# A fused FFT filter and squared-ReLU feed-forward kernel: the last zeta tile split, its last rows read alone, a cast shared by three engines, and one more group in the plain product form

## The chip, the cores and the metric

The kernel runs on one core of a Trainium2 chip. The metric is the device time of one launch in microseconds (us). Inputs and the output lie in the chip's main memory (DRAM) in fp32; the kernel computes in fp16 with fp32 sums in PSUM. Below, PE is the matrix engine, PEld its weight loads, DVE the vector engine, ACT the scalar (activation) engine, POOL the GpSimd engine and SP the engine that issues most transfers (DMA).

## What is computed

```python
X = np.fft.rfft(x, axis=1)                       # x: 8 x 3008 x 256
y = np.fft.irfft(X * (filt_r + 1j*filt_i), n=3008, axis=1)
h = np.maximum(y.reshape(24064, 256) @ w_in, 0)  # w_in: 256 x 2048
out = (h * h) @ w_out                            # w_out: 2048 x 256
```

## The kernel before, in words

**The filter part** goes batch by batch (8 batches). The FFT of 3008 = 64 x 47 points is done as matmuls in stages. `unit_a` (line 332; for batch 0 `unit_a0` and `turn_u`) makes u; for batches 1 to 7 it is written to DRAM (`write_u`) and read back turned (`read_u`). `unit_b` (line 406) makes a spectrum tile and DVE multiplies it by the filter `sF` (line 421). `unit_p` (line 454; for batch 0 `unit_p0`, line 435) transforms back to "zeta", which is cast to fp16, written to DRAM (`dZ`) and read back by `read_z` (line 475) in four chunks c, into two tiles `zt` that take turns. `unit_y` (line 483) makes the tokens `yt` of the feed-forward part.

**The feed-forward part** goes through 47 groups of 512 tokens, in 8 slots each: a loop over s at line 809. In its slots 8g to 8g+7 group g runs `ffn_g1` (the first product: 4 matmuls of 128x512 a slot, line 527, followed by an ACT ReLU of 128x1024, line 531) and `ffn_sq` (DVE squares of 128x2048 every second slot, line 538). In the eight slots that follow, the second product is made in one of two forms. The plain form, `ffn_g2` and `ffn_out`, has per slot 8 matmuls of 128x256 (line 547) and two ACT copies of the result a group. The other form, used for the groups in `SEVEN` (line 806) and run one slot later, saves multiplications in the manner of Strassen and Winograd: 112 matmuls of 128x128 (`products`, line 642) on blocks and on sums of blocks. DVE makes four sums of 128x2048 a group (`sums`, lines 613 to 622) and adds three results (lines 657 and 663); ACT copies four. It needs four differences of blocks of w_out, made once by `make_t` (line 594) in slots 12 to 15.

**The order of the work.** Each engine takes its instructions in the order in which the program gives them; it is written out by hand. Lines 734 to 804 are the prologue: batch 0 through the filter up to the first `unit_y`. After it, `fft_plan` (line 668) lays the units of batches 1 to 7 onto half-slots of the loop, with due times in slots. SP's transfers keep their program order too: in the prologue the zeta writes (line 450), then `read_z(0, 0)` and `read_z(0, 1)`, then eight writes of u of batch 1, each put there by `unit_a(1, c)`, then `read_z(0, 2)`. POOL loads w_out (line 321) only after a tiny copy (line 792) that reads the first row of the first zt tile.

**The filter's way in.** The two parts of the filter come as fp32 of 128x3008; each is cast to fp16 in two halves by DVE and POOL (lines 756 and 763). `place_f` (line 269) turns four rows at a time into `sF` with matmuls and one or two casts. For the imaginary part its block 0 (`place_f(1, 0, ...)`, line 768) reads columns 0 to 1023 and 2240 to the end.

**PSUM** is shared by three tags of two buffers each: `psH` (1024 fp32 wide, two banks), `psF` and `psO` (512 wide, one bank each). A new tile of a tag waits until the tile two before it has been read out. `unit_b`, `unit_p` and (after the prologue) `unit_y` all take `psF`.

**The last zeta of batch 0.** `unit_p0(5)` makes four rows of 128 in one psH tile and casts them in three pieces (line 447): rows 0 and 1 by ACT, row 2 by ACT, row 3 by DVE, each followed by its write to DRAM. `unit_a(1, 0)` follows on PE. Before the first `unit_y` there are five matmuls that only fill time (line 799).

Of the kernel before, what the change touches and what calls it, by code (L numbers as in the profile page):

```python
# [22 lines left out]
QF = 3008  # L23
# [87 lines left out]
def kernel(  # L111
# [9 lines left out]
    nc = tc.nc  # L121
    B, S, D = x.shape
# [5 lines left out]
    NG = T // TG  # L128
# [28 lines left out]
    def psF(name):  # L157
        return pps.tile([128, 512], F32, tag="psF", name=name, bufs=2)

    def psO(name):  # L160
        return pps.tile([128, 2, 256], F32, tag="psO", name=name, bufs=2)

    def psH(name):
        return pps.tile([128, 2, 512], F32, tag="psH", name=name, bufs=2)
# [4 lines left out]
    def bank_pair(name):  # L169

        k = npair[0] % 4
        npair[0] += 1
        if k < 2:
            t = psH(name)
            return [t[:, 0, :], t[:, 1, :]], [(t, 0)]
        ts = [psF(f"{name}_{i}") if k == 2 else psO(f"{name}_{i}").rearrange("p a d -> p (a d)")
              for i in range(2)]
        return ts, [(t.unsqueeze(1), i) for i, t in enumerate(ts)]
# [5 lines left out]
    x16s, us, uts, prods, zes, zts, yts = {}, {}, {}, {}, {}, {}, {}  # L184
# [36 lines left out]
    def cast(eng, out, in_):  # L221
        (eng.copy if eng is nc.scalar else eng.tensor_copy)(out=out, in_=in_)
# [9 lines left out]
    f32s = []  # L232
# [17 lines left out]
    sSP = const.tile([128, NC, 128], F16, name="sSP")  # L250
# [12 lines left out]
    ps = psO("warm").rearrange("p a d -> p (a d)")  # L263
# [3 lines left out]
    f16s = []  # L267

    def place_f(im, k, *engs, rotate=False):

        if rotate:
            banks, groups = bank_pair(f"psf_{im}_{k}")
        else:
            t = psH(f"psf_{im}_{k}")
            banks, groups = [t[:, 0, :], t[:, 1, :]], [(t, 0)]
        for i in range(4):
            c = 4 * k + i
            e0, e1 = D * c, D * (47 - c)
            cuts = [0] + [d for d in range(1, D)
                          if (e0 + d) % QF == 0 or (c and (e1 + d) % QF == 0)] + [D]  # L280
            for d0, d1 in zip(cuts, cuts[1:]):
                o = banks[i // 2][:, (i % 2) * D + d0:(i % 2) * D + d1]
                low = divmod(e0 + d0, QF)
                up = divmod(e1 + d0, QF) if c else (0, QF + d0)
                for r, (q, a) in enumerate((low, up, low, up)):
                    nc.tensor.matmul(o[32 * r:32 * r + 32, :], sPF[:, q, :],
                                     f16s[0][:, im, a:a + d1 - d0], start=True, stop=True)
        for t, i in groups:
            n = t.shape[1]
            eng = engs[i % len(engs)]  # L290
            dst = sF[:, im, 4 * k + 2 * i:4 * k + 2 * i + 2 * n, :]
            src = t.rearrange("p t (a d) -> p (t a) d", d=D)
            if eng is nc.scalar:
                eng.activation(out=dst, in_=src, func=AF.Copy, scale=sign[:, 0:1] if im else 1.0)
            elif im:
                eng.tensor_scalar_mul(out=dst, in0=src, scalar1=sign[:, 0:1])
            else:
                eng.tensor_copy(out=dst, in_=src)
# [33 lines left out]
    def unit_a(b, c):  # L332

        pool, tag = (p_y, "yt") if (b, c) == (1, 3) else (p_u, "u")
        u = us[(b, c)] = pool.tile([112, 8, D], F16, tag=tag, name=f"u_{b}_{c}")
        ph = psH(f"psA_{b}_{c}")
        if b == 1 and c % 2:
            ps = [psO(f"psA_{b}_{c}_{h}").rearrange("p a d -> p (a d)") for h in range(2)]
        else:
            ps = [psF(f"psA_{b}_{c}_{h}") for h in range(2)]  # L340
        for i in range(2):
            for j in range(2):
                m = slice(4 * j + 2 * i, 4 * j + 2 * i + 2)
                for h in range(2):
                    p = slice(64 * h, 64 * h + N2)
                    o = ps[h] if i == 0 else ph[:, h, :]
                    nc.tensor.matmul(o[64 * j:64 * j + 64, :], sSA[p], x16s[(b, c)][p, m, :],  # L347
                                     start=True, stop=True)
        for h in range(2):
            o = u[:, h:h + 3:2, :]  # L350
            pv = ps[h][0:112, :].rearrange("p (e d) -> p e d", d=D)
            if h == 0 or b == 1:
                nc.scalar.copy(out=o, in_=pv)
            else:
                nc.vector.tensor_copy(out=o, in_=pv)
        o = u[:, 4:8, :].rearrange("p (e h) d -> p h e d", h=2)
        pv = ph[0:112].rearrange("p h (e d) -> p h e d", d=D)
        if b == 1:
            nc.vector.tensor_copy(out=o, in_=pv)
        else:  # L360
            nc.scalar.copy(out=o, in_=pv)
        if b == 1:
            write_u(b, c)
# [69 lines left out]
    sSPx = []  # L433

    def unit_p0(k):

        if k == 0:
            zes[0] = p_h2.tile([128, NC, D], F16, tag="h2", name="ze_0")
        ze = zes[0][:, 4 * k:4 * k + 4, :]
        ps = psH(f"psP_0_{k}")  # L440
        for i in range(4):
            c2 = 4 * k + i
            prod = prods[(0, c2 // 2)]
            for v, w in enumerate((sSP[:, c2, :], sSPx[c2 // 12][:, c2 % 12, :])):
                nc.tensor.matmul(ps[:, i // 2, (i % 2) * D:(i % 2) * D + D], w,
                                 prod[:, v, i % 2, :], start=(v == 0), stop=(v == 1))
        for i, (c0, c1) in enumerate(((0, 4),) if k < 5 else ((0, 2), (2, 3), (3, 4))):
            cast(nc.vector if i == 2 else nc.scalar, ze[:, c0:c1, :],
                 ps.rearrange("p t (a d) -> p (t a) d", d=D)[:, c0:c1, :])
            nc.sync.dma_start(  # L450
                out=dZ[0].rearrange("(s p) d -> p s d", p=128)[:, 4 * k + c0:4 * k + c1, :],
                in_=ze[:, c0:c1, :])
# [22 lines left out]
    def read_z(b, c, ks=(0, 1)):  # L475
        zt = ztiles[c % 2]
        v = dZ[b].rearrange("(q j) d -> q j d", j=NM)
        for k in ks:
            nc.sync.dma_start(out=zt[64 * k:64 * k + 48],
                              in_=v[48 * k:48 * k + 48, 8 * c:8 * c + 8, :])  # L480
        zts[(b, c)] = zt

    def unit_y(b, n):
# [101 lines left out]
    def make_t(k):  # L585

        w = sWout.rearrange("p (q e) c -> p q e c", e=2)
        b11, b12 = w[:, :, 0, 0:128], w[:, :, 0, 128:256]
        b21, b22 = w[:, :, 1, 0:128], w[:, :, 1, 128:256]
        if k == 0:  # L590
            sg["t"] = p_t.tile([128, 4, 8, 128], F16, tag="t", name="sT")
        t = sg["t"]
        i0, i1 = ((b12, b11), (b22, t[:, 0]), (b22, b12), (b21, t[:, 1]))[k]
        nc.vector.tensor_sub(out=t[:, k], in0=i0, in1=i1)
        sg["w"] = {1: b11, 2: b21, 3: b22, 4: t[:, 3], 5: t[:, 0], 6: t[:, 1], 7: t[:, 2]}
# [133 lines left out]
    def run(plan, s, place):  # L729
        for f, *a in plan.get(2 * s + place, ()):  # L730
            f(*a)
# [7 lines left out]
    for k in range(2):  # L739
        c = slice(12 * k, 12 * k + 12)  # L740
# [19 lines left out]
    turn_u(4, nc.scalar)  # L760
    turn_u(5, nc.vector)
    place_f(0, 0, nc.scalar, rotate=True)
    for eng, e in ((nc.vector, slice(0, 1504)), (nc.gpsimd, slice(1504, QF))):
        cast(eng, f16s[0][:, 1, e], f32s[1][:, e])
    place_f(0, 1, nc.vector, rotate=True)
    for k in (2, 3):
        place_f(0, k, nc.scalar, rotate=True)
    place_f(1, 0, nc.scalar, nc.vector, rotate=True)
    for k in range(6):
        if k % 3 == 0:  # L770
            sSPx.append(p_u.tile([128, 12, 128], F16, tag="u", name=f"sSPx_{k}"))
        c, o = slice(4 * k, 4 * k + 4), slice(4 * k % 12, 4 * k % 12 + 4)
# [22 lines left out]
    for c in range(4):  # L795
        unit_a(1, c)
    ps = psF("fill")
    for _ in range(5):
        nc.tensor.matmul(ps, zero, sSB[:, 0:4, :].rearrange("p a b -> p (a b)"),
                         start=True, stop=True)  # L800
# [2 lines left out]
    prologue[0] = False  # L803
    read_z(0, 2)

    SEVEN = range(1, NG - 1)
    work = fft_plan()

    for s in range((NG + 1) * SLOTS):
        g, k = divmod(s, SLOTS)  # L810
        if g < NG:
            ffn_g1(g, k)
        run(work, s, 0)
        if 12 <= s < 16:
            make_t(s - 12)
        if (s - 1) // SLOTS - 1 in SEVEN:
            products((s - 1) // SLOTS - 1, (s - 1) % SLOTS, s)
        if g > 0 and g - 1 not in SEVEN:
            ffn_g2(g - 1, k)
        run(work, s, 1)  # L820
        if g > 0 and g - 1 not in SEVEN:
            ffn_out(g - 1, k)
        if g - 1 in SEVEN:
            sums(g - 1, k)
        if g < NG:
            ffn_sq(g, k)
        while stores and stores[0][0] <= s:
            _, i, n, ost = stores.pop(0)
            store(i, n, 2, ost)
# [30 lines left out]
```

## Time and profile before

| | us |
|---|---|
| device time, median of 3 | 757.33 (755.15 to 759.18) |
| profiled execution, span | 754.4 |
| PE busy | 737.1 (98%) |
| DVE busy | 651.0 (86%) |
| ACT busy | 563.5 (75%) |
| POOL busy | 192.2 (25%) |

Busy time is what the profiler has recorded for an engine. The matmuls are pipelined, so that the record of one lies over the start of the next: 8 matmuls of line 547 show 1.04 us, and the next work starts 0.87 to 0.88 us after them. Where PE's work is counted below, the distance from start to start is used. An entry in square brackets in a timeline is the idle time ahead of it and what ended it.

### The profile page before, as it was taken

What the parts mean: (1) busy time and instruction counts of PE and PEld (TensorE: products, weight loads), DVE (VectorE), ACT (ScalarE), POOL (GpSimd) and SP (SyncE); (2) the same over time, 40 slices, a digit from 0 to 9 for tenths busy, and PEclk for the clock granted to TensorE, in tenths of its full rate; (3) what the DMA queues carried; (4) which work ended last, traced back from release to release, by engine and by line L of the source; (5) the groups of instructions that cost most, each with busy time, mean ns of one, the idle gap of its engine ahead of it and who ended that gap; (6) DMA issues with size and microseconds to landing.
All of it is one profiled execution on the core that took longest, in us unless ns stands there. A gap on an engine that the chain in (4) does not pass through costs nothing.

```text
span 754.4 us, 20080 instructions
## 1 busy us (share of the span) xinstructions
PE 737.1 (98%) x8455; PEld 535.6 (71%) x8455; DVE 651.0 (86%) x724; ACT 563.5 (75%) x805; POOL 192.2 (25%) x265
## 2 busy tenths in 40 slices
PE   7889999999999999999999999999999999999998
PEld 5536667767677777877778776787778777777776
DVE  5956998899899897999979998999989989888783
ACT  5876787787778777777777778777787777777773
POOL 2811650243222321232304224033311222000000
PEclk9999999999999999999999999999999999999999
DMA  9996898566795557656585646764447333321011
GB/s 348 309 200 183 146 178 245 142 120 120 162 237 111 104 120 183 173 106 137 103 226 124 125 98 138 231 128 101 105 118 203 73 82 88 100 85 43 29 58 56
DMA packets 103490, 106.34 MB, mean 141 GB/s; under 512 B 10352, under 2 KB 93552, under 8 KB 102248
## 3 DMA queue, kind: packets, MB, share of 16 engines
q1 hardware_dynamic: 83960, 81.83, 36.0%
q0 software_dynamic: 19296, 23.05, 21.6%
q8 instruction: 66, 1.08, 0.6%
q10 hardware_dynamic: 144, 0.18, 0.2%
q14 instruction: 24, 0.20, 0.1%
HBM read 57.80 MB, written 48.23 MB: 141 GB/s over the span
## 4 chain that ended last, share of the span: by engine, by line
PE 87%; DMA 6%; DVE 3%; ACT 1%; issue 1%; POOL 1%; SPq 0%; DVEq 0%
PE psH L527 40%; PE psX L642 20%; PE psY L642 16%; PE psY L497 3%; PE psB L412 2%; PE psP L461 2%; DMA f<-in_filt_i_dram 2%; PE psA L347 2%; DVE prod L421 1%; DMA zt<-dZ 1%; PE psO L547 1%; DMA prod<-prod 1%; DMA dZ<-ze 1%; DVE h L538 1%; DMA sC<-cC 1%
## 5 line engine op out<-in xcount | busy, mean ns | idle before, releaser
L531 ACT ACTIVATE h<-psH 128x1024 f16<-128x1024 f32 x376 | 385.4, 1026 | 161.1 <-PE psH L527 160.1
L527 PE MATMUL psH<-yt,sWin 128*128 128x512 f16 (+7 forms) x1728 | 387.0, 351 | 1.2 <-ACT h L531 0.4
L538 DVE TENSOR_TENSOR h<-h 128x2048 f16<-128x2048 f16 (+1 forms) x192 | 229.9, 1198 | 47.6 <-ACT h L531 45.1
L429 POOL DMA_DIRECT2D prod<-prod x168 | 138.8, 968 | 427.6 <-DVE prod L421 425.3
L527 PEld LDWEIGHTS <-sWin 128*128 128x128 f16 x1728 | 149.2, 98 | 90.4 <-issue 3.0
L642 PEld LDWEIGHTS <-sum 128*128 128x128 f16 x2880 | 177.4, 98 | 24.8 <-issue 5.3
L642 PEld LDWEIGHTS <-h 128*128 128x128 f16 x2160 | 132.6, 98 | 24.3 <-issue 5.3
L421 DVE TENSOR_TENSOR prod<-psB,sF 128x1024 f16<-128x1024 f32 x84 | 102.3, 1219 | 12.6 <-PE psB L412 12.5
L642 PE MATMUL psX<-sT,sum 128*128 128x128 f16 x1440 | 102.4, 219 | 0.0
L642 PE MATMUL psY<-sT,sum 128*128 128x128 f16 x720 | 69.7, 219 | 0.0
L195 POOL DMA_DIRECT2D x<-in_x_dram x64 | 55.9, 1045 | 0.5 <-PE psA L347 0.5
L616 DVE TENSOR_TENSOR sum<-sum,h 128x2048 f16<-128x2048 f16 x45 | 54.9, 1221 | 0.8
L642 PE MATMUL psY<-sWout,sum 128*128 128x128 f16 x720 | 54.7, 219 | 0.6 <-DVE bot L657 0.6
L642 PE MATMUL psY<-sWout,h 128*128 128x128 f16 x720 | 55.0, 219 | 0.0
L642 PE MATMUL psX<-sT,h 128*128 128x128 f16 x720 | 54.9, 219 | 0.0
L619 DVE TENSOR_TENSOR sum<-h 128x2048 f16<-128x2048 f16 x45 | 54.8, 1217 | 0.0
L622 DVE TENSOR_TENSOR sum<-h,sum 128x2048 f16<-128x2048 f16 x45 | 54.8, 1217 | 0.0
L613 DVE TENSOR_TENSOR sum<-h 128x2048 f16<-128x2048 f16 x45 | 54.7, 1216 | 0.0
L463 ACT CAST ze<-psP 128x512 f16<-128x512 f32 x84 | 49.1, 585 | 1.1 <-PE psP L461 0.9
L506 DVE CAST yt<-psY 128x376 f16<-128x376 f32 x62 | 33.7, 544 | 16.7 <-PE psY L497 16.5
L642 PE MATMUL psX<-sWout,h 128*128 128x128 f16 x720 | 47.7, 219 | 0.0
L497 PE MATMUL psY<-sC,zt 112*128 112x94 f16 x512 | 42.3, 204 | 1.8 <-DVE prod L421 1.2
(76 smaller groups left out, 557.2 us busy)
## 6 DMA issues: line engine op xcount, KB each, us to landing
zt<-dZ SPq DMA_DIRECT2D x64, 192.0 KB
dU<-u SPq DMA_DIRECT2D x56, 192.0 KB
prod<-prod POOLq DMA_DIRECT2D x168, 64.0 KB, 2.7
dZ<-ze SPq DMA_DIRECT2D x28, 384.0 KB
x<-in_x_dram POOLq DMA_DIRECT2D x48, 192.0 KB, 5.0
ut<-dU SPq DMA_DIRECT2D x7, 1024.0 KB
out_dram<-top SPq DMA_DIRECT2D x31, 128.0 KB
out_dram<-bot SPq DMA_DIRECT2D x31, 128.0 KB
```

Source lines behind the costliest of these rows:

```text
L195: nc.gpsimd.dma_start(out=t[64 * h + p0:64 * h + p1], in_=v[p0:p1, 8 * c:8 * c + 8, :])
L421: nc.vector.tensor_mul(out=prod[:, :, a:a + n, :], in0=ps.rearrange("p (a d) -> p a d", d=D)[:, a:a + n, :].unsqueeze(1) .to_broadcast([12 ...
L429: nc.gpsimd.dma_start(out=prod[64 * i:64 * i + 64, 0], in_=prod[64 - 64 * i:128 - 64 * i, 1], accum_op=mybir.AluOpType.add)
L497: nc.tensor.matmul(ps[:, 94 * jj:94 * jj + 94], zt[:, 4 * (g % 2) + jj, dt * 128:(dt + 1) * 128], sSY, start=True, stop=True)
L527: nc.tensor.matmul(ps[:, i, o:o + n], sWin[:, dt, jt * 128:(jt + 1) * 128], yts[b][:, dt, r:r + n], start=(dt == 0), stop=(dt == 1))
L531: nc.scalar.activation(out=h2[:, 2 * s:2 * s + 2, :], in_=ps, func=AF.Relu)
L538: nc.vector.tensor_mul(out=v, in0=v, in1=v)
L613: nc.vector.tensor_add(out=t, in0=a21, in1=a22)
L616: nc.vector.tensor_sub(out=t, in0=f[5], in1=a11)
L619: nc.vector.tensor_sub(out=t, in0=a11, in1=a21)
L622: nc.vector.tensor_sub(out=t, in0=a12, in1=f[6])
L642: nc.tensor.matmul(o[:, t, :], f[p][:, q, 128 * t:128 * t + 128], sg["w"][p][:, q, :], start=(m == 0 and p in (1, 2)), stop=(q == 7), skip ...
```

## The change

It has four parts.

1. **The last zeta in three tiles.** In `unit_p0(5)` the three pieces get PSUM tiles of their own: rows 0 and 1 a psH tile, rows 2 and 3 a psF tile each. Each piece's cast follows its own matmuls. As this takes two psF tiles, `unit_a(1, c)` swaps: even c now take psO, odd c psF.
2. **The last z rows alone.** `read_z(0, 0)` reads rows 0 to 47, 48 to 79 and 80 to 95 in three transfers. Only the last depends on what `unit_p0(5)` writes. The other reads stay in two.
3. **The imaginary filter's cast in three parts.** POOL's half (columns 1504 to 3007) is cut at 2496, and ACT casts the rest, between two of its `place_f` casts.
4. **Group 1 in the plain form.** `SEVEN` starts at 2, so that groups 0 and 1 use w_out itself. The four differences of `make_t` move from slots 12 to 15 to slots 20 to 23.

```diff
-        if b == 1 and c % 2:
+        if b == 1 and c % 2 == 0:
             ps = [psO(...) for h in range(2)]
         else:
             ps = [psF(...) for h in range(2)]
...
-        ps = psH(f"psP_0_{k}")
-        for i in range(4):
...
-        for i, (c0, c1) in enumerate(((0, 4),) if k < 5 else ((0, 2), (2, 3), (3, 4))):
-            cast(nc.vector if i == 2 else nc.scalar, ze[:, c0:c1, :],
-                 ps.rearrange("p t (a d) -> p (t a) d", d=D)[:, c0:c1, :])
+        pieces = ((0, 4),) if k < 5 else ((0, 2), (2, 3), (3, 4))
+        pss = []
+        for c0, c1 in pieces:
+            if c1 - c0 > 1:
+                ps = psH(f"psP_0_{k}").rearrange("p t (a d) -> p (t a) d", d=D)
+            else:
+                ps = psF(f"psP_0_{k}_{c0}").rearrange("p (a d) -> p a d", d=D)
+            pss.append(ps)
+            for i in range(c0, c1):
...
+        for i, (c0, c1) in enumerate(pieces):
+            cast(nc.vector if i == 2 else nc.scalar, ze[:, c0:c1, :], pss[i][:, 0:c1 - c0, :])
...
-        for k in ks:
-            nc.sync.dma_start(out=zt[64 * k:64 * k + 48],
-                              in_=v[48 * k:48 * k + 48, 8 * c:8 * c + 8, :])
+        for q0, q1 in ((0, 48), (48, 80), (80, 96)) if (b, c) == (0, 0) else ((0, 48), (48, 96)):
+            r = q0 + q0 // 48 * 16
+            nc.sync.dma_start(out=zt[r:r + q1 - q0], in_=v[q0:q1, 8 * c:8 * c + 8, :])
...
-    for eng, e in ((nc.vector, slice(0, 1504)), (nc.gpsimd, slice(1504, QF))):
+    for eng, e in ((nc.vector, slice(0, 1504)), (nc.gpsimd, slice(1504, 2496))):
         cast(eng, f16s[0][:, 1, e], f32s[1][:, e])
     place_f(0, 1, nc.vector, rotate=True)
-    for k in (2, 3):
-        place_f(0, k, nc.scalar, rotate=True)
+    place_f(0, 2, nc.scalar, rotate=True)
+    cast(nc.scalar, f16s[0][:, 1, 2496:QF], f32s[1][:, 2496:QF])
+    place_f(0, 3, nc.scalar, rotate=True)
...
-    SEVEN = range(1, NG - 1)
+    SEVEN = range(2, NG - 1)
...
-        if 12 <= s < 16:
-            make_t(s - 12)
+        if 20 <= s < 24:
+            make_t(s - 20)
```

More of the change, by code (lines that the diff above doesn't have):

```diff
@@ L439, in unit_p0 @@
         ze = zes[0][:, 4 * k:4 * k + 4, :]
-        ps = psH(f"psP_0_{k}")
-        for i in range(4):
[L442 to L446, printed above, removed]
-        for i, (c0, c1) in enumerate(((0, 4),) if k < 5 else ((0, 2), (2, 3), (3, 4))):
-            cast(nc.vector if i == 2 else nc.scalar, ze[:, c0:c1, :],
-                 ps.rearrange("p t (a d) -> p (t a) d", d=D)[:, c0:c1, :])
+        pieces = ((0, 4),) if k < 5 else ((0, 2), (2, 3), (3, 4))
[7 more added lines that the diff above has]
+            for i in range(c0, c1):
+                c2 = 4 * k + i
+                prod = prods[(0, c2 // 2)]
+                for v, w in enumerate((sSP[:, c2, :], sSPx[c2 // 12][:, c2 % 12, :])):
+                    nc.tensor.matmul(ps[:, i - c0, :], w, prod[:, v, i % 2, :],
+                                     start=(v == 0), stop=(v == 1))
+        for i, (c0, c1) in enumerate(pieces):
+            cast(nc.vector if i == 2 else nc.scalar, ze[:, c0:c1, :], pss[i][:, 0:c1 - c0, :])
             nc.sync.dma_start(
```

## The prediction

> **What bounds the kernel now.** I first read the page's shares, then busy time by stretch, to see where PE has slack.
>
> ```profile
> core 0: us, PE busy (x) PEld busy (x) DVE busy (x) ACT busy (x) POOL busy (x), PEclk, DMA share, GB/s
> 44.00:62.00 18.00, 16.08 (x104) 8.26 (x102) 9.09 (x10) 11.40 (x14) 2.01 (x3) 0.94 1.02 200
> 62.00:76.00 14.00, 13.77 (x111) 9.33 (x110) 9.87 (x13) 9.37 (x13) 4.26 (x6) 1.00 0.63 177
> 76.00:103.00 27.00, 24.97 (x268) 17.60 (x266) 26.52 (x27) 20.19 (x31) 16.67 (x23) 1.00 0.90 162
> 103.00:120.00 17.00, 17.00 (x194) 11.32 (x193) 14.77 (x17) 15.05 (x23) 5.39 (x8) 1.00 0.91 202
> ```
>
> From 103 us PE is full, and it stays so (100.00 of 100.00 us in each stretch of 100 from 200 to 700). So only what happens ahead of 103 us can be gained, and PE work added anywhere is paid. Ahead of 103 there are two losses. From 76 to 103 DVE is the full engine. Before 62 a chain of waits binds; the chain by time for 36 to 63 shows it:
>
> ```profile
> 38.67 0.39 PE psP L445 x2
> ...
> 39.09 0.86 ACT ze L222 x2
> 39.95 0.50 ACT u L353
> 40.45 0.34 SPq L450
> ...
> 40.88 1.83 DMA dZ<-ze
> ...
> 42.80 3.24 DMA zt<-dZ
> ...
> 46.18 0.33 PE psY L497 x4
> ...
> 55.05 7.25 DMA zt<-dZ
> ```
>
> The last zeta's casts begin only when its last matmul is done, its third piece is written at 40.88, and the last read of z (192 KB) takes 3.24 us after that. The same chain starts, in time order from 0, with the imaginary filter landing at 20.77, then POOL's cast to 23.05. The timelines of POOL, DVE and PE give the rest:
>
> ```profile
> 15.65 1.44 POOL L222 CAST f<-f 128x1504 f16<-128x1504 f32 x1 [2.21 <-DMA f<-in_filt_r_dram]
> 20.82 2.21 POOL L222 CAST f<-f 128x1504 f16<-128x1504 f32 x1 [3.73 <-DMA f<-in_filt_i_dram]
> 39.98 0.43 DVE L222 CAST ze<-psP 128x256 f16<-128x256 f32 x1 [1.36 <-ACT ze L222]
> 43.29 2.32 PE L799 MATMUL fill<-sSB,zero 128*128 128x512 f16 x5
> 60.32 1.03 PE L547 MATMUL psO<-sWout,h 128*128 128x256 f16 x8 [0.48 <-DMA sWout<-in_moe_w_out_dram]
> 82.44 0.33 PE L497 MATMUL psY<-sC,zt 112*128 112x94 f16 x4 [1.01 <-DVE prod L421]
> ```
>
> POOL's second cast is 0.77 longer than its first, the third zeta piece waits for ACT's cast of the second, and at 82.44 PE stands waiting for a DVE product.
>
> [...] rows 2 and 3 share a bank, and DVE waited 1.36. [...] the 64 KB write of zeta took 1.83 on SP's. [...] Here the clock is 0.50 in each us from 43 to 46, and the five fill matmuls take 2.32.
>
> **The change part by part.**
>
> *Filter cast, −0.5.* POOL's 992 columns cost 1.44 x 992/1504 = 0.95, after the same 0.77 wait: done at 22.54, not 23.03. ACT's 128x512 is not in the trace from SBUF; the nearest row, from PSUM, is 0.59, and two full rows would be 1.03 at most. It queues behind `place_f(0,2)`'s cast and ahead of `place_f(0,3)`'s, so ACT reaches `place_f(1,0)` at 20.43 + 0.97 + 0.5 + 0.97 = 22.87 (start to start), against 23.42 before. DVE and ACT then run without gaps to 38 us, so 0.5 is passed on (0.3 with the dearer ACT cast).
>
> *Zeta tiles, −1.3.* Rows 0 and 1 (matmuls at 37.48) and row 2 (38.08) are cast while PE does row 3 (38.67 to 39.05); DVE casts row 3 at 39.09 and not 39.98. Its write is issued near 39.55 instead of 40.88, where SP had just spent 0.34 on piece two. With the filter's 0.5 it is near 39.05, 1.8 earlier, and lands near 40.9 (42.71).
>
> *Last z rows, up to −0.8 more.* The last read is 64 KB, not 192: between 1.83 (the write of this size) and 3.24; I take 2.4. z is there near 43.4 (46.04). The added transfer costs SP about 0.4 to issue. Queued behind it are `read_z(0,1)` and the u writes, first at 44.13, now near 42.2: still 1.9 earlier.
>
> *What can use it.* PE must first do `unit_a(1,c)` and the fill. DVE's four casts of u (4.61 from 40.32) begin 1.3 earlier, which puts the fill at 42.0 to 42.3 (43.29), the first `unit_y` near 44.9 (46.18): 1.3 gained, 2.4 if the clock stays up and the fill takes 1.1. The swap of psO and psF makes the fill wait for ACT's seventh copy of u, near 42.25: hidden under that. From 57.3 to 62.44 PE waits for transfers: its work there is 0.65 + 2 x 0.87 of line 527 and 2 x 0.875 of line 547, 4.1 of 5.1. These transfers (w_out, started by the tiny copy after the first zt read, which moves from 41.36 to about 39.4; z of chunk 2, behind the u writes) begin 1.9 earlier. So at 62.4 the gain is the 1.9 of the transfers: PE's 1.3 and its slack of 1.0 cover it. **Front: −1.9** (1.0 to 2.5).
>
> *Group 1 plain.* PE: 64 matmuls, 8 in 0.875, are 7.0; the 112 removed, 16 in 0.89, were 6.23. **+0.77**, on the path. DVE loses 4 sums at 1.13 (start to start) and 3 adds at 0.33: −5.5 of the 26.5 between 76 and 103. ACT loses four copies at 0.38 and gains two of 0.59: −0.35, hidden. The differences (4 x 0.60 = 2.4) leave 67 to 75 and come at about 83 to 91; the first reader is in slot 26, near 96. DVE's work from 76 to 93 falls from 16.8 to 13.7, below PE's.
>
> *What that frees.* I count PE's work from 75.86 to 103.28 start to start: 12 x 0.866 (line 527), 3 x 0.17 (`unit_y`), 8 x 0.22 (`unit_b`), 7 x 0.22 (`unit_p`), 0.56 (`unit_a`) and 172 x 0.0556 (products) are 24.3 of 27.4: 3.1 lost. Of these, 1.17 stand before 82.44, 0.35 before 91.04, 0.63 before 102.90, 0.34 in two smaller places: 2.5 by DVE. The 0.58 before 77.33 waits for ACT after slot 16, which has no second product; this hole moves to slot 24, and I let half of it go. Freed 2.5 + 0.28 = 2.8, less 0.77: **−2.0** (+0.5 to −2.4).
>
> Sum: −1.9 − 2.0 = −3.9; 757.33 − 3.9 = 753.4.
>
> **The rivals.** *All of it works* (22%): PE stays at full clock (front 2.5) and all 3.1 come back (2.3): 752.5. For it: the matmuls before the fill stand closer. Against: PE's busy time from 36 to 44 hardly grows. *Half clock takes the place of the z wait* (13%): a half-clock window of 3.4 us, which cost nothing at 43 to 46 since z was awaited, falls on the first two slots of group 0, where PE and ACT take turns. Four matmuls then take 1.73 for 0.87; some 1.3 of 1.9 are lost: 754.7. [...] *DVE stays the bound* (12%): the moved differences meet DVE's products; of 2.8 only 1.3 come back, front whole: 757.33 − 1.9 − 0.5 = 754.9. Against: 13.7 of 17 us. *Slower* (7%): the swapped PSUM tags and the extra transfer eat the front, two half-clock windows fall into group 0 (6.8 us at half speed, 3.4 lost), and the plain form costs its 0.77 with nothing freed: 757.33 + 4.2 = 761.5. Against: four things must go wrong together.
>
> **How the numbers follow.** The likeliest case, 753.4, has 46%. Half a per cent is 3.8, so it lies at the line: with the scatter of the three times (757.33 −2.2 +1.9) I give it 6 in 10 to be below. Faster: 0.28 + 0.22 + a little of the middle cases = 0.52. Slower 0.07. Same 0.41. The range goes from the best case less 1.3 of scatter, 751.2, to the two middle cases with as much on top, 756.3; the slower case and half of what strays from the middle ones stay outside.
>
> **What would show it.** In the profile after: POOL's second f cast near 1.7; three zeta casts of which DVE's no longer waits for ACT; first `unit_y` at 43.5 to 45; z of chunk 2 near 60.4 instead of 62.3; no PE wait on line 421 between 74 and 100; PE full from about 99.5. Wrong if PE is full only from 102 or later: then the clock row at 42 to 50 and the waits on line 421 say which half failed.

## The result and the profile after

The changed kernel takes 754.66 us (median of 22 runs, 752.85 to 757.44) against 756.17 (22 runs, 754.68 to 759.18). The ratio is 0.9979, with a 95% interval of 0.9971 to 0.9987. It is faster by about 1.6 us by the ratio (1.5 by the medians), where the prediction had 3.9. The profiled execution spans 752.3 us (754.4 before).

The same stretches as in the prediction, now of the kernel after:

```profile
core 0: us, PE busy (x) PEld busy (x) DVE busy (x) ACT busy (x) POOL busy (x), PEclk, DMA share, GB/s
44.00:62.00 18.00, 15.37 (x110) 8.35 (x108) 8.71 (x10) 11.48 (x16) 2.01 (x3) 1.00 1.02 208
62.00:76.00 14.00, 14.00 (x113) 9.74 (x111) 9.27 (x10) 9.34 (x12) 5.59 (x7) 1.00 0.62 169
76.00:103.00 27.00, 26.46 (x242) 18.54 (x239) 24.73 (x25) 21.63 (x32) 17.48 (x26) 1.00 0.93 170
103.00:120.00 17.00, 16.84 (x193) 10.98 (x192) 13.81 (x16) 15.46 (x23) 3.28 (x6) 1.00 0.93 215
```

From 76 to 103 us PE has gone from 24.97 to 26.46 of 27 and is the full engine. This half went much as expected. The front (the work ahead of about 62 us) did not. The chain of waits between 36 and 63 us:

```profile
38.77 0.87 ACT ze L222 x2
...
40.37 3.03 DMA dZ<-ze
...
43.47 3.02 DMA zt<-dZ
...
46.53 0.34 PE psY L503 x4
```

The third zeta write is issued 0.51 earlier than before (40.88), but it takes 3.03 us where it took 1.83. The last read takes 3.02, although it moves 64 KB and not 192 (3.24). The first `unit_y` is at 46.53, which is 0.35 later than before (46.18). The timelines of POOL, DVE and PE, row by row:

```profile
20.61 1.80 POOL L222 CAST f<-f 128x992 f16<-128x992 f32 x1 [3.48 <-DMA f<-in_filt_i_dram]
39.73 0.42 DVE L222 CAST ze<-psP 128x256 f16<-128x256 f32 x1 [0.47 <-PE psP L452]
43.64 1.24 PE L806 MATMUL fill<-sSB,zero 128*128 128x512 f16 x5 [0.52 <-ACT u L353]
46.53 0.34 PE L503 MATMUL psY<-sC,zt 112*128 112x94 f16 x4 [1.54 <-DMA zt<-dZ]
100.66 0.38 PE L467 MATMUL psP<-prod,sSP 128*128 128x256 f16 x2 [0.54 <-DVE prod L421]
```

POOL's cast is shorter. DVE's zeta cast no longer waits for ACT but for PE, as planned. The fill has full clock (1.24 for 2.32). One PE wait for DVE is left, at 100.66. Where did the half clock go? The third number from the right is the granted clock, in one stretch of 1 us (it is 0.50 in the two after it as well):

```profile
24.00:25.00 1.00, 1.00 (x17) 0.49 (x17) 0.83 (x1) 0.01 (x1) 0.96 (x3) 0.50 1.05 398
```

In this execution the window fell at 23.9 to 27.3 us, on the `place_f` and spectrum matmuls, and the last zeta matmul came at 39.43 (38.78 before), though the first spectrum matmul had come at 23.59 (24.16). In the profile of before the window fell where PE waited for z (42.60 to 46.01; z landed at 46.04), and cost nothing.

The offsets below are the start of a slot's first line-527 (533) matmul, less its start in the profile of before:

| kernel | slot 11 | slot 25 | slots 11 to 25 | end |
|---|---|---|---|---|
| prediction | −1.9 | −3.9 | −2.0 | −3.9 |
| after | −0.65 | −2.31 | −1.66 | −2.07 |

Half-clock windows vary from run to run, so a single profile says little on the end time, or on the front: e3 below, whose front is that of before, is at −1.07 at slot 11. Each run also lists the span on the core and its mean granted clock; one window of 3.4 us at half clock takes some 0.002 (1.7 of 752) off that mean. By this estimate, of the 22 runs of after 10 had no window (mean span 752.11), 10 had one (753.30) and 2 more than one (755.10). So one costs about 1.2 us. Below, means of these spans are given where medians are too coarse; for before they are 754.5 to 754.8 (17 to 59 runs). The kernel before has such windows too: only 12 of the 59 runs taken beside e1 to e4 had none, and these are at 753.71, beside 754.54 for all 59. The windows take 0.8 from the mean of either kernel, and in the runs without one the change gains 1.6 as well.

### The profile page after: what moved, and what is told of

Same layout as the page of the kernel before. It is cut to its first block, busy times and chain, and to the rows that moved or that the text cites. A ratio compares the mean times of both kernels' runs of the same rounds, so it can differ in the third digit from the quotient of the medians.

```text
span 752.3 us, 19976 instructions
## 1 busy us (share of the span) xinstructions
PE 736.8 (98%) x8407; PEld 535.4 (71%) x8407; DVE 645.9 (86%) x717; ACT 563.7 (75%) x804; POOL 191.6 (25%) x265
## 3 DMA queue, kind: packets, MB, share of 16 engines
q8 instruction: 66, 1.08, 0.6%
## 4 chain that ended last, share of the span: by engine, by line
PE 91%; DMA 3%; DVE 2%; ACT 1%; issue 1%; SPq 0%; DVEq 0%; ACTq 0%
PE psH L533 41%; PE psX L648 20%; PE psY L648 15%; PE psO L553 3%; PE psB L412 3%; PE psY L503 3%; PE psP L467 2%; PE psA L347 2%; DMA zt<-dZ 1%; DMA xw<-in_x_dram 1%; DMA dZ<-ze 1%; PE psf L286 1%; ACT h L537 1%; PE psP L452 1%; DVE prod L421 0%
## 5 line engine op out<-in xcount | busy, mean ns | idle before, releaser
L544 DVE TENSOR_TENSOR h<-h 128x2048 f16<-128x2048 f16 (+1 forms) x192 | 229.6, 1197 | 48.5 <-ACT h L537 48.1
L648 PEld LDWEIGHTS <-sum 128*128 128x128 f16 x2816 | 173.4, 98 | 24.7 <-issue 5.3
L648 PEld LDWEIGHTS <-h 128*128 128x128 f16 x2112 | 129.6, 98 | 24.1 <-issue 5.4
L648 PE MATMUL psX<-sT,sum 128*128 128x128 f16 x1408 | 100.1, 219 | 0.0
L648 PE MATMUL psY<-sT,sum 128*128 128x128 f16 x704 | 68.1, 219 | 0.0
L625 DVE TENSOR_TENSOR sum<-h 128x2048 f16<-128x2048 f16 x44 | 53.5, 1215 | 0.0
L619 DVE TENSOR_TENSOR sum<-h 128x2048 f16<-128x2048 f16 x44 | 53.4, 1214 | 0.0
```

The source lines that it names most:

```text
L544: nc.vector.tensor_mul(out=v, in0=v, in1=v)
L619: nc.vector.tensor_add(out=t, in0=a21, in1=a22)
L625: nc.vector.tensor_sub(out=t, in0=a11, in1=a21)
L648: nc.tensor.matmul(o[:, t, :], f[p][:, q, 128 * t:128 * t + 128], sg["w"][p][:, q, :], start=(m == 0 and p in (1, 2)), stop=(q == 7), skip ...
```

## The experiments

**e1: part 4 alone** (group 1 plain, differences moved).

```diff
-    SEVEN = range(1, NG - 1)
+    SEVEN = range(2, NG - 1)
-        if 12 <= s < 16:
-            make_t(s - 12)
+        if 20 <= s < 24:
+            make_t(s - 20)
```

> The fourth part alone: group 1 in the plain form and the differences in slots 20 to 23, on the kernel before. Theory A (the whole gain is the plain form; the front gives nothing at the mean): 1.2 to 2.0 us faster than before, PE waits on line 421 gone between 74 and 98, one near 100 left. Theory B (the front gives about half): 0.5 to 1.0 faster.

**e2: parts 1 to 3 alone.** The kernel after with `SEVEN = range(1, NG - 1)` and `make_t` in slots 12 to 15.

> Parts one to three without the fourth. Theory A: within 0.5 us of before, since the last read of z lands no earlier (about 46) although it is a third of the size. Theory B: 0.7 to 1.5 faster. Prediction on record: 1.9 faster.

**e3: as e1, with the differences left in slots 12 to 15.**

```diff
+    SEVEN = range(2, NG - 1)
         if 12 <= s < 16:
             make_t(s - 12)
```

> Group 1 plain, the four differences left in slots 12 to 15. If the 5.5 us of sums and adds taken from DVE are what frees PE: the same as the fourth part alone within 0.4 us. If moving the 2.4 us of differences matters: 0.5 to 1.0 us slower than that.

**e4: part 3 alone** (the filter's cast in three).

> The cast of the imaginary filter in three parts alone. If its 0.5 us reaches the first unit_y: 0.3 to 0.5 faster. [...] the first spectrum matmul near 23.6 instead of 24.16 either way.

| | us | ratio [95%] | mean span |
|---|---|---|---|
| e1 plain | 755.58 | 0.9995 [0.9986, 1.0003] | 753.75 |
| e2 front | 755.71 | 0.9996 [0.9985, 1.0007] | 754.04 |
| e3 plain, early differences | 755.70 | 0.9995 [0.9984, 1.0006] | 753.96 |
| e4 filter | 755.83 | 0.9997 [0.9990, 1.0005] | 754.25 |

Alone, no part can be told from no change. By mean span e1 gains 0.8 (its theory B) and e2 0.5, together 1.3, which is within the scatter of the 1.6 of all four. In the trace the plain form does its work at once: slots 11 to 25 give −1.62 in e1 and −1.42 in e3. So whether the differences move hardly matters. But at the end only −1.34 (e1) is left of −1.95 at slot 25. The PE timeline of e1 shows where it goes:

```profile
574.19 0.33 PE L497 MATMUL psY<-sC,zt 112*128 112x94 f16 x4 [0.43 <-DMA zt<-dZ]
```

This is the first `unit_y` of batch 6's third chunk. Before, it started at 575.51 without a wait. PE, now nearly 2 us ahead, reaches it before the z read has landed. A gain made at 100 us runs into a later transfer.

In e2 the front itself shows two things, in the chain and in the busy time by stretch:

```profile
39.26 3.08 DMA dZ<-ze
42.41 3.24 DMA zt<-dZ
45.69 0.49 PE psY L503 x4
```

```profile
46.00:49.00 3.00, 2.95 (x24) 1.99 (x22) 1.10 (x2) 0.94 (x2) 0.00 (x0) 0.50 1.04 169
```

The write is issued 1.62 earlier than before, near the 39.05 predicted, but write and read take 3.08 and 3.24, and the first `unit_y` gains 0.49. Then the half-clock window falls on group 0, which is the second rival of the prediction. In e4 the first spectrum matmul gains 0.41 (23.75), then two windows undo it.

**e5: part 1 alone** (three tiles; the last read keeps its 192 KB). **e6: part 2 alone** (the 64 KB read, one psH tile).

> The last zeta in three PSUM tiles, with the swap of psF and psO, nothing else. DVE's cast of the third piece starts near 39.1 instead of 39.98, its write is issued near 39.6 instead of 40.88. Theory F or Q: the landing takes 2.5 to 3.1 instead of 1.83, so that it is near 42.4 and the first unit_y gains 0.3 at most. Prediction on record: lands 1.3 earlier.

> The last z rows read alone, nothing else. If the read is bound by its bytes: 64 KB land 1.0 to 1.4 us sooner than the 192 KB of before (3.24 from issue to the first unit_y's release). If by latency: 3.0 to 3.3 as before, and the first unit_y no earlier than 46.

One run each: 756.30 and 756.26 us. In e5 the third write is issued at 39.52 and lands 3.30 later; its read of 192 KB takes 3.18. In e6 the write is issued at 41.75, the 64 KB read at 43.41, and `unit_y` starts about 3.0 later, with PE waiting:

```profile
46.45 0.34 PE L497 MATMUL psY<-sC,zt 112*128 112x94 f16 x4 [0.94 <-DMA zt<-dZ]
```

So in these runs the small read is no faster than the large one, with or without part 1. And part 1 alone is enough for the slow write.

**e8: group 2 plain too** (after, `SEVEN = range(3, NG - 1)`, differences in slots 28 to 31).

> The changed kernel with group 2 plain as well, the differences in slots 28 to 31. PE pays 0.77 more; DVE loses another 5.5 us between 90 and 105, where it is full in the changed kernel and PE waits 0.7 at 100.6. If this wait is the whole loss there: 0 to 0.3 slower than the changed kernel. If DVE holds PE in more places: 0.5 or more faster.

755.77 us, 0.9987 [0.9978, 0.9997]; mean span 753.58, 0.66 above after. The DVE wait at 100.66 is gone and PE is full:

```profile
76.00:103.00 27.00, 27.00 (x211) 18.73 (x209) 19.18 (x17) 20.30 (x29) 17.55 (x25) 1.00 0.91 166
```

DVE has nearly 8 us of slack, and nothing is left for it to free: the 0.77 us of PE work that a plain group costs buys 0.54 of waits, a loss of 0.23. The profile shows two more losses against after: one `unit_a` at 111.9 takes 0.31 more, and the `unit_y` at 120.83 waits 0.41 for z of batch 2 (0.16 in after, at 119.08). From slot 11 to slot 40 e8 loses 0.87 to after in all. The forecast of 0 to 0.3 left these two out. A second plain group doesn't pay here.

**e9: the same fill at the start in smaller matmuls.** In the packets of the trace, an instruction fetch shows amid the zeta writes of after: one packet of 16384 bytes at 40.49, which takes 1.353 us. The writes' packets are of 512 bytes and mostly take 0.027 each. The last 32 of them run one behind another, as on a single engine, from 41.84, where the fetch ends, to 42.87; the others are over by then. The packets don't name their engine; that it is the one with the fetch is read from these times. The page of after counts 66 packets, 1.08 MB, on this queue (q8, instruction).

The page also counts 16814 matmuls and weight loads on PE (8407 of each). If the queue brings PE's instructions, that is one packet for about 255 of them, an estimate from these two counts. Adding PE instructions at the start, in the same time, must then bring the packet at 40.49 earlier:

```diff
-    for _ in range(WARM):
-        nc.tensor.matmul(ps, zero, sF[:, 0, 0:2, :], start=True, stop=True)
+    for _ in range(4 * WARM):
+        nc.tensor.matmul(ps[:, 0:128], zero, sF[:, 0, 0, 0:128], start=True, stop=True)
```

> The changed kernel, with the ten warm-up matmuls of 128x512 replaced by forty of 128x128 (same PE time, 60 more PE instructions), so that PE's 16 KB instruction fetch, at 40.5 in the changed kernel, comes about 2.5 us earlier, out of the way of the last zeta writes. Theory F (the fetch holds one DMA engine for 1.35 us, and the last write lands late because of that engine): the last write lands 1.8 to 2.2 us after its issue instead of 3.0, the last z read is issued near 41, the first unit_y 0.5 to 1.0 us earlier than in the changed kernel. Theory Q (the writes only queue behind one another): the landing stays near 3.0.

754.62 us, 0.9975 [0.9965, 0.9986]; mean span 752.85. The fetch is now at 36.4, ahead of the third write (39.97), which lands in about 2.2 us; the first `unit_y` is at 44.57, 1.61 ahead of before (part of this is that the profile of e9 has no half-clock window). But the mean is that of after. By slot 11 only −1.05 is left, because of the transfer next in line:

```profile
59.65 1.03 PE L553 MATMUL psO<-sWout,h 128*128 128x256 f16 x8 [1.39 <-DMA sWout<-in_moe_w_out_dram]
```

Over all kernels, the time from the third write's issue to the last read's (which waits for it):

| | kernels | us |
|---|---|---|
| fetch during the write | after, e2, e5, e8 | 3.1, 3.15, 3.4, 2.9 |
| fetch over, three tiles | e7, e9, e10, e11 | 2.4, 2.2, 2.2, 3.1 |
| fetch over, one tile | before, e1, e3, e4, e6, e12 | 1.9, 1.9, 1.9, 1.7, 1.7, 1.7 |

Each write leaves 16 landing marks in the trace (events that say that a part has landed), as many as the DMA engines of which the page gives shares; the write is done with the last (43.40 in after, 3.03 behind its issue). In all 14 kernels 13 of the third write's 16 marks have come by 1.54 to 1.62 us after its issue, with one tile or three. The table's differences lie in the last three. With the fetch in it the last mark comes 1.2 to 1.7 behind the thirteenth: in after and e8 it is a single late mark, which fits a fetch that holds one engine; in e2 and e5 two more are late beside it. Without, it comes 0.3 or less behind in the one-tile kernels, 0.5 to 0.75 in e7, e9 and e10, and 1.4 in e11. The single late mark is thus taken to be that of the fetch's engine: the last packets go on where the fetch ends (41.84), and with the fetch moved (e9) no mark is so late. What held the others isn't shown.

**e10: as e9, with chunk 2's z read ahead of the last four u writes.**

```diff
-        if b == 1:
+        if b == 1 and c < 2:
             write_u(b, c)
...
     read_z(0, 2)
+    for c in (2, 3):
+        write_u(1, c)
```

> The fetch-shift kernel with the read of z's chunk 2 moved ahead of the last four of the eight u writes on SP. There PE is 1.6 us ahead of before at slot 8, and 1.4 of it are lost waiting for the second half of w_out (landed 59.61). Theory T (the transfers between 44 and 62 share the DMA engines and are what takes back the front's gain): with four u writes behind it, w_out lands near 58, PE keeps 1.3 or more at slot 11, and the mean is 0.5 to 0.8 us under the fetch-shift kernel. Rival (the w_out load has its own pace): it lands near 59.6 as before and nothing is gained.

754.60 us, 0.9980 [0.9973, 0.9987]; mean span 752.82. w_out still makes PE wait 0.43, at 59.12. The front keeps −1.58 at slot 11 and −3.24 at slot 25, but PE then waits 1.1 us at the same `unit_y` of batch 6, and −1.93 is left. The mean missed its forecast of 0.5 to 0.8 under e9's: in the profile, the z read of batch 6 takes back what is above some 2 us.

**e7: filling matmuls that keep the clock up.** Three behind `place_f(1, 0)`, four in the tiles of `unit_p0(5)`; their results are overwritten or not read.

```diff
     place_f(1, 0, nc.scalar, nc.vector, rotate=True)
+    ps = psH("warm2")
+    for _ in range(3):
+        nc.tensor.matmul(ps[:, 0, :], zero, f16s[0][:, 0, 0:512], start=True, stop=True)
...
             pss.append(ps)
+            for _ in range(2 if k == 5 and c0 < 3 else 0):
+                nc.tensor.matmul(ps.rearrange("p a d -> p (a d)")[:, 0:512], zero,
+                                 f16s[0][:, 0, 0:512], start=True, stop=True)
```

> The changed kernel with seven more matmuls of 128x512 that only fill PE's waits near 23 and between 37 and 39. Theory C (half-clock windows of 3.4 us in the front cost about 1.2 us each where they fall on needed work, and fall less often when PE is busier): fewer runs with such a window than the changed kernel's 12 of 22, mean 0.3 to 0.6 us lower. Rival (the fill does not change the windows, or delays PE by itself): same mean within 0.3, or 0.3 slower.

754.25 us, 0.9968 [0.9959, 0.9977]; mean span 752.23. 12 of 14 runs are without a half-clock window (10 of 22 in after). These 12 are at 752.24 and after's 10 at 752.11, so by these means what e7 gains on after is the windows. In its profile the fetch has moved as well (37.23 to 38.56, ahead of the third write), so its front isn't due to the clock alone. It is the front as predicted: the last zeta matmul at 38.25, the first `unit_y` at 44.41, and in the chain

```profile
39.58 2.35 DMA dZ<-ze
42.00 2.36 DMA zt<-dZ
```

−2.20 at slot 11 and −3.30 at slot 25. Then, on PE and on SP's queue:

```profile
573.88 0.33 PE L506 MATMUL psY<-sC,zt 112*128 112x94 f16 x4 [1.44 <-DMA zt<-dZ]
```

```profile
560.88 0.89 SPq L403 DMA_DIRECT2D ut<-dU  x2
561.81 2.13 SPq L589 DMA_DIRECT2D out_dram<-top  x3
563.98 6.63 SPq L489 DMA_DIRECT2D zt<-dZ  x4
```

The z read that PE waits for is the first pair of these four, issued at 563.98 and 564.76, behind the whole u read of the last batch, 1.5 MB, on the same queue. Its last landing mark is at 573.75.

**e11: as e7, with the u read of batches 3 to 7 cut in two**, the larger part behind the z read of the batch before.

```diff
-                moves.append((f + (2 if b == 2 else -6.5), read_u, b))
+                if b == 2:
+                    moves.append((f + 2, read_u, b))
+                else:
+                    moves.append((f - 6.5, read_u, b, (0,)))
+                    moves.append((f + 1, read_u, b, (1,)))
```

> This kernel is the one of e7 (all four parts and the filling matmuls), with the u read of each batch from the fourth on cut in two: the first 8 of its 24 pieces stay where they were, the other 16 are issued behind the z read of the previous batch's last chunk. Theory (that z read is late because 1.5 MB of u are queued ahead of it): the first unit_y of batch 6's third chunk, which waited 1.44 us at 573.88, starts without a wait over 0.3 us, TensorE keeps the 3.3 us that it is ahead of the kernel before at slot 25, the span ends 2.7 to 3.3 us ahead instead of 1.7, and the mean core span is 0.7 to 1.4 us under e7's 752.2. Rival (something else sets the landing, such as the instruction fetches in that window): the same unit_y still starts between 573.5 and 574.2 with a wait of 1 us or more, and the mean is within 0.3 of e7's. A third way: the second part of the u read comes late for its batch, and a wait on u appears at the start of a batch; then the mean is above e7's.

753.40 us (5 runs, 752.37 to 753.72), 0.9960 [0.9947, 0.9972]; mean span 751.34, so 0.9 under e7's, as expected, though with 5 and 14 runs the intervals of the two ratios overlap. In the trace it is plain. PE and SP at the same place:

```profile
571.76 0.33 PE L507 MATMUL psY<-sC,zt 112*128 112x94 f16 x4
```

```profile
560.38 0.34 SPq L405 DMA_DIRECT2D ut<-dU  x1
...
562.28 7.82 SPq L490 DMA_DIRECT2D zt<-dZ  x4
```

The read is now issued at 562.28 and 562.84, with only the first 0.5 MB of u ahead of it (the other 1 MB goes at 572.86), and lands at 568.18. There is no wait, −3.77 at slot 25 stays, and the end is at −3.81. This is the fastest kernel here: about 3.0 us (0.40%) under before.

**e12: the kernel before with e7's filling alone.**

> This kernel is the one before, without any part of the change, with e7's filling matmuls alone (3 behind the first filter placement, 4 in the fifth unit_p tile's first two pieces). Theory (the half-clock window costs what it hits, about 1 us, and the change brings its 1.6 us beside that): 0.3 to 0.8 us faster than before, a ratio of 0.9990 to 0.9996, well under e7's 2.4 us. Rival (e7's gain is mostly the filling, and the change brings little): 1.5 us or more faster, a ratio of 0.9980 or less. If the filling brings nothing by itself, since the kernel before has its half-clock window where TensorE waits anyway: within 0.3 us of before.

755.88 us, 0.9991 [0.9983, 1.0000]; mean span 754.20 beside before's 754.79. The filling by itself brings some 0.6, and the change alone 1.6; e7's 2.4 is about their sum. Beside this kernel, which has the filling as well, e11 gains 2.9 by mean span.

## Why the prediction was right in direction and too large in size

That the measured 754.66 stands only 1.3 above the likeliest 753.4 is luck in part: the prediction started from 757.33, the median of three runs, where the 22 runs have 756.17. The gain is off by 2.3 to 2.4. That 754.66 meets the half-clock rival's 754.7 is chance for the same reason. Of the signs named, those on POOL's cast, on DVE's zeta cast and on line 421 came; the first `unit_y` at 43.5 to 45 did not (46.53), and z of chunk 2 landed at 60.82 (near 60.4 named).

**Filter cast, −0.5: right.** The first spectrum matmul came 0.57 earlier. ACT's cast of 128x512 took 0.61 as recorded and 0.51 to the next start (0.5 taken). POOL's took 1.80 and not 0.95 + 0.77 = 1.72. In both profiles it ran beside DVE's cast of 128x1504 (0.94 before, 0.93 after); what adds to POOL's time isn't shown.

**Zeta tiles, −1.3: right for the issue of the write, wrong for its landing.** In e2, without a window ahead of it, the write was issued at 39.26, 1.62 earlier (1.8 predicted with the filter's part). "lands near 40.9" took the 1.83 of before for a write with nothing close ahead of it. It measured 3.08, and 3.03 in after: 13 of the 16 landing marks had come by 1.62, as before, but one to three were late, one of them taken to be behind the fetch. The prediction had no term for other work on the DMA engines.

**Last z rows, "I take 2.4": right in half of the profiles.** To its last landing mark the 64 KB read took 3.02, 3.24, 2.99 and 2.98 in after, e2, e6 and e8, and 2.36, 2.34, 2.56 and 2.38 in e7, e9, e10 and e11; the 192 KB read took 3.18 to 3.48 in six kernels. In after 15 of the 16 marks were there after 2.02, the last one 1.00 later. Two fetch packets of 8192 bytes, 43.98 to 45.11, fall into this read and may have held that mark back; no run tests it.

**The half clock: given 13% and present in about half the runs (12 of 22).** The prediction reckoned with a window on group 0 (it came in e2), but in the profile of after it fell on the spectrum matmuls, ahead of the last zeta. The filter's earlier cast doesn't prevent it; e7's fill nearly does (12 of 14 runs have none). But in the means the kernel before loses the same 0.8 to its windows, so they don't explain why the change gained 1.6 and not 3.9.

**Front, −1.9 at 62.4: the sum was right, its input not.** The prediction let PE's gain at the first `unit_y` and a slack of 1.0 decide, bounded by the transfers. After: −0.35 + 1.0 = 0.65, measured 0.65. e11: 1.26 + 1.0 = 2.26, measured 2.26. e7: 1.77 + 1.0 = 2.77, held by the z read of chunk 2 to 2.20. e9: held by w_out to 1.05. But the transfers didn't begin 1.9 earlier: w_out was issued at 44.85 (44.49 before) and the first write of u at 45.34 (44.13). The second half of w_out landed at 57.41 all the same (60.28), and z of chunk 2 at 60.82 (62.30); in e3, with the front of before, they came at 58.75 and 61.23. So these landings did not follow their start, and what set them isn't shown.

**Plain form, −2.0: right in mechanism, −1.1 to −1.7 in size** (after 1.66, e1 1.62, e3 1.42, e7 1.10, e11 1.51). No PE wait on line 421 is left from 74 to 98. The 0.63 at 102.90 was counted as freed, but it remains as 0.54 at 100.66, since group 2's sums follow there. The rival "DVE stays the bound" is out, by the stretch 76 to 103.

**The full PE from 103 us, taken to keep whatever is gained ahead of it: wrong as a step.** It was true of the kernel before, but only while PE came no earlier. From about 2 us on, the z read of batch 6 can be late: e7 lost 1.66 after slot 25, e10 1.31, e3 0.85, e1 0.6. The read's landing varies: in after it came at 572.49 and this `unit_y` started at 573.52 without a wait, while in e1, with the same lead of 1.9, it came at 574.05. Of after's −2.31 at slot 25, 0.37 went by slot 40, most of it in the slot of the wait for z of batch 2 at 119.08.

With these losses taken away (clock, fetch, z read) e11 ends at −3.81 in its profile, near the −3.9 of the prediction, and some 3.0 [2.1, 4.0] in its times. But 0.6 of this is the filling's, which before gains as well (e12). So of the 3.9 some 2.9 are shown in the means; what the remaining 1.0 is stays open. Cutting the u read alone, without the change, was not run.

The steps that failed are thus the landing of the third write and of the read behind it, priced without a term for a late landing mark (3.03 for 1.83, 3.02 for 2.4 in after), and the full PE from 103 us, taken as proof that a lead stays.

## What to carry to other kernels

Ahead of a chain of small transfers, ask what else uses the same DMA engines and queue at the new time, not only what the transfer took at the old one: its duration is not its own (the third write took 1.83 us before and 3.03 after). After a gain, follow PE to the end of the kernel with the new lead and look for each transfer with less slack than that lead; here one 1.5 MB read, queued ahead of a smaller urgent one, capped the profiles of e1, e3, e7, e9 and e10 at 1.3 to 2.1 us. And where a stage has short gaps on PE, judge an edit of 1 us by many runs and by the granted clock of each, since one half-clock window (1.2 us) is nearly as large as the effect (1.6).

## What the runs showed of the hardware that was not expected

- By the times of the packets, instruction fetches share DMA engines with data: in after the last 32 packets of the zeta writes ran one behind another from 41.84, where the fetch ended, and with the fetch moved (e9) the last mark of the third write was 0.5 to 0.75 behind the thirteenth and not 1.2 to 1.7. In e11 it was 1.4 behind with the fetch over, so the fetch is not the only cause. Near that write, the fetch packets of 16384 bytes took 0.88 to 1.52 us. The time from its issue to the last read's was 2.9 to 3.4 us with a fetch in it, 1.7 to 1.9 without in the one-tile form and 2.2 to 3.1 in the three-tile form. Thirty more matmuls at the start, with their weight loads, moved the fetch from 40.49 to 36.39.
- The time of a small transfer was that of its last landing mark. Of the third write's 16 marks 13 had come by 1.54 to 1.62 us after the issue in every kernel, the last by 1.6 to 3.3. A read of 64 KB straight after the write that it waits for took 2.34 to 3.24, one of 192 KB 3.18 to 3.48.
- Half-clock windows in the front lasted 3.4 us (6.8 in e5) and came at 23.9 to 25.0 or at 42.5 to 48.5 us, or not at all. One cost nothing where PE waited anyway (the profile of before), and about 1.2 us in the mean over the runs of after. In the 3.4 us just ahead of them PE had been busy for 1.2 to 2.8 us (1.98 in after, 2.32 in before), so what came just before them was no idle stretch; what starts a window isn't shown. Seven added matmuls took the share of runs without one from 10 of 22 to 12 of 14 (3 of 5 in e11, which has them too), and in the kernel before from 12 of 59 to 6 of 13 (e12).
